# The numerators of six tile pairs move from the banks of the queries and transposes to the banks of the row maxima

## The chip, the core and the metric

The kernel runs on one core of a Trainium2 chip. A core has a matrix engine (TensorE, in the profile PE, with its weight loads as PEld), a vector engine (VectorE, DVE), a scalar engine (ScalarE, ACT), a general engine (GpSimd, POOL) and a queue that issues transfers (SyncE, SP). Each engine works through its own list of instructions in order, and waits at an instruction until the semaphores that it names are set. TensorE writes its products into accumulator tiles of 128 partitions by 512 f32 values, called banks here; ScalarE and VectorE read them out.

The metric is device time in microseconds (us) of one execution. Of the kernel before there are three runs: 979.75, 980.02 and 980.48 us.

## The reference: what is computed

Two attention layers work on the same 2048 tokens of 448 features, with 16 heads of 28 features, and a gate per token mixes them:

```python
g = sigmoid((x * gate_w).sum(-1, keepdims=True))
a = A(x)     # linear attention with a learned feature map
b = B(x)     # ordinary softmax attention
return g * a + (1 - g) * b
```

Layer A turns each query and key by a 28 x 28 matrix per head and takes softmax of the result and of its negative, which gives 56 features. With these, `kv = phi_k^T v` and `z = sum(phi_k)` are formed once per head; the output of a query is the numerator `phi_q kv` divided by the denominator `phi_q z`, and goes through `wo`. Layer B is softmax(q k^T / sqrt(28)) v, also through its `wo`.

## The kernel before

The work goes through stages, all in f32; products that need the precision are built from a high and a low part in the faster f32r format.

1. Projection of layer B's queries and keys, written to DRAM (`proj_qk`), up to about 100 us.
2. Key stage of layer A: for each of 16 tiles of 128 tokens, keys, features and values, and their sum over tokens in `pkv`.
3. Query stage of layer A, about 185 to 325 us. This is where the change lies.
4. Values of layer B (`value_b`), up to about 355 us.
5. Attention of layer B to the end: 256 steps of scores, exponentials and values.

Beside stages 2 to 4, TensorE also forms a part of layer B's scores in 80 units (`mx_unit`), only to find the largest score of each row: a softmax of layer B subtracts it later.

**The query stage.** One loop (`for i in range(2 * NT + 11)`) goes over the tiles; `q = i - 16` counts the query tiles and `y = q - 1`. The engines PE, DVE, ACT and POOL run in exactly the order in which the code issues; the order of SP's transfers is chosen by a planner when the program is built. In one turn of the loop these steps matter, in this order on TensorE:

- `pq`: the projection of query tile q, 11 products into one bank (`tok_major`, called at line 127 or 109 of the profile; here 109). ScalarE copies it out as `pcq` (L421). VectorE and GpSimd make the features `featq` from it.
- `mx_unit()` for q of 0, 1 and from 8 on: four products (L260, `pmd` and `pmb`, two of each) into four banks. ScalarE takes the positive part of the two `pmd` banks into `rl` (L264), and VectorE adds the two `pmb` banks to these and takes the maximum (L265). The two `pmd` banks are free after L264, the two `pmb` banks after L265.
- `numer(tb)` in every second turn, for tile pair tb = 0 to 7 (q = 5, 7, ..., 19): 32 small products (L529) into two banks `pn_0` and `pn_1`, written in turns: the first product goes to `pn_0`, the second to `pn_1`, and so on. ScalarE copies both out as `oUa` (L381, in `normalize1`).
- `turn`: eight transposes `pft` of features (L516) into two banks, copied out by ScalarE as `fT` (L519).
- `out_a`: 12 products `poa` (L109) for an earlier tile, copied out by ScalarE as `ga` (L544) and sent to DRAM as `gad` (L545). The order of `turn` and `out_a` changes late in the stage.

A numerator's division takes several turns: a small transfer `dena` (L384) collects the denominators from `oUa`, VectorE inverts them (L389), two small transfers write them to DRAM as `rda` (L393), and one of 512 KB spreads them over the partitions as `rsa` (L394). VectorE multiplies (L400), ScalarE and GpSimd split the result into `oTa` (L408, L409), which `poa` reads.

**The banks.** In the query stage there is one pool of banks, `psq`, with two rotations of four each:

```python
def ps_s(nm):
    return ps.tile([P, 512], F32, tag="s", name=nm, bufs=psn[0])
def ps_mx(nm):
    return ps.tile([P, 512], F32, tag="mx", name=nm, bufs=psn[1])
```

`psn` is 4 and 4 in this stage. The rotation `s` serves `pq`, `pft`, `pn`, `poa` and later `pvb`; the rotation `mx` serves only `mx_unit`, whose four tiles take all four of its banks, in the order pmd_0, pmd_1, pmb_0, pmb_1. A new tile takes the bank of the tile allocated four before it in its rotation, and its first product waits until that bank has been read out.

Of the kernel before, what the change touches and what calls it, by code (L numbers as in the profile page):

```python
# [41 lines left out]
def gated_mix_kernel(ctx, tc, xT, wqkB, wvB, wvA, wkAT, wqAT, phi, woA, woB,  # L42
# [20 lines left out]
    def ps_s(nm):  # L63
        return ps.tile([P, 512], F32, tag="s", name=nm, bufs=psn[0])
# [312 lines left out]
    def normalize1(pool, pn, nm, n):  # L377

        oU = pool.tile([P, n, 512], F32, tag="oU", name=f"oU{nm}", bufs=2 * n - 1)
        for i in range(n):  # L380
            (nc.scalar.copy if n == 2 else nc.vector.tensor_copy)(oU[:, i, :], pn[i])  # L381
        den = pool.tile([P, n, 16], F32, tag="den", name=f"den{nm}", bufs=2)
        for i in range(n):
            nc.sync.dma_start(den[:, i, :], oU[DH:P:32, i, :])  # L384
        return oU, den
# [135 lines left out]

    def numer(tb):

        pn = [ps_s(f"pn{tb}_{i}") for i in range(2)]
        for k in range(2):
            for j in range(4):
                for e in range(2):
                    es = slice(64 * e, 64 * e + 2 * DH + 1)
                    nc.tensor.matmul(pn[e][32 * j:32 * j + 32, k * 256:(k + 1) * 256],  # L529
                                     KV[es, k, 32 * j:32 * j + 32], fT_of[tb][es, 4 * k + j, :],  # L530
                                     start=True, stop=True, tile_position=(64 * e, 32 * j))
        num[tb] = normalize1(ta, pn, f"a{tb}", 2)
# [170 lines left out]
    for i in range(2 * NT + 11):  # L703
        t, q = i, i - NT
        y = q - 1
        tb = y // 2
# [80 lines left out]
        if y >= 4 and y % 2 == 0 and tb - 2 < 8:  # L787
            numer(tb - 2)
# [455 lines left out]
```

## Time and profile before

| | |
|---|---|
| median of three runs | 980.02 us (979.75 to 980.48) |
| the profiled execution | 979.64 us |
| its span in the trace | 977.9 us |
| PE busy | 970.2 us (99%) |
| ACT busy | 751.8 us (77%) |
| DVE busy | 715.9 us (73%) |
| POOL busy | 227.4 us (23%) |

Times in the trace are counted from the start of the span. A row of the timeline names its start, its length, engine, line, operation, what it writes and reads, and how many instructions it merges; in square brackets stands the idle time of that engine just before, and what ended it. The end of a product is modelled, so a short wait of TensorE is seen best at its weight loads (PEld): each product has a weight load of its own, in the same order.

### The profile page before, as it was taken

The page shows a single profiled execution, that of the slowest core. Times are in us where ns is not written, and L with a number is a line of the kernel's source. Part 1 is how long each engine was busy: PE and PEld are TensorE (multiplying, and loading weights), DVE is VectorE, ACT ScalarE, POOL GpSimd, SP SyncE. Part 2 cuts the span into 40 slices and gives each one's busy share as a digit, 9 for nine tenths or more (in the row PEclk, how much of TensorE's full clock was granted, in tenths as well). Part 3 has the DMA queues.
Part 4 walks back from the last instruction along what each step waited for, and adds up shares of the span by engine and source line. Part 5 has one row for each costly group of instructions (what it writes and reads, how often), then busy time and mean ns, then how long its engine had stood idle before and what let it go on. Part 6 is the DMA issues. An engine that isn't in the chain of part 4 may idle for free.

```text
span 977.9 us, 22543 instructions
## 1 busy us (share of the span) xinstructions
PE 970.2 (99%) x8510; PEld 600.8 (61%) x8510; DVE 715.9 (73%) x1338; ACT 751.8 (77%) x1442; POOL 227.4 (23%) x236
## 2 busy tenths in 40 slices
PE   9999999999999999999999999999999999999998
PEld 8877877787777655555555555555555555555555
DVE  5566767789745678888888888888888888885112
ACT  4455655578865689888898898988989889887662
POOL 1135435577634800021011001011011011010010
PEclk9999999999999999999999999999999999999999
DMA  9873110112243333022132121122231222100441
GB/s 305 310 256 113 39 53 33 37 52 82 75 114 108 98 112 132 29 59 50 60 91 73 33 61 47 59 77 72 65 83 45 63 60 64 42 21 32 142 151 57
DMA packets 56140, 84.49 MB, mean 86 GB/s; under 512 B 17216, under 2 KB 23984, under 8 KB 56032
## 3 DMA queue, kind: packets, MB, share of 16 engines
q1 hardware_dynamic: 56032, 83.06, 28.0%
q8 instruction: 67, 1.10, 0.5%
q14 instruction: 41, 0.34, 0.1%
HBM read 54.86 MB, written 27.78 MB: 85 GB/s over the span
## 4 chain that ended last, share of the span: by engine, by line
PE 93%; DMA 3%; DVE 2%; issue 1%; ACT 1%; SPq 1%; POOL 0%; DVEq 0%; POOLq 0%; ACTq 0%
PE g L863 29%; PE pv L1008 27%; PE pqk L109 5%; PE pk L127 4%; PE pva L127 4%; PE g L288 3%; PE poa L109 3%; PE pmd L260 3%; PE pob L109 3%; PE pq L109 3%; PE pvb L127 2%; PE pvb L109 2%; DMA rsa<-rda 2%; PE pqk L630 1%; PE pkv L468 1%
## 5 line engine op out<-in xcount | busy, mean ns | idle before, releaser
L871 ACT ACTIVATE p<-g 128x512 f32<-128x512 f32 x1020 | 525.6, 608 | 82.7 <-PE g L863 82.4
L295 DVE TENSOR_REDUCE part<-g 128x1 f32<-128x512 f32 x704 | 442.2, 683 | 84.0 <-PE g L288 82.8
L863 PEld LDWEIGHTS g<-qst,kst 32*128 32x128 f32 x3060 | 220.8, 182 | 215.5 <-DVE part L295 194.9
L863 PE MATMUL g<-qst,kst 32*128 32x512 f32 x3060 | 337.6, 419 | 0.1
L1008 PE MATMUL pv<-p,vb 128*32 128x512 f32 x2048 | 273.0, 604 | 0.0
L288 PE MATMUL g<-kc,qc 28*128 28x512 f32 x704 | 233.3, 494 | 0.0
L265 DVE CUSTOM_DVE_ANT_0 rl<-pmb,rl 128x512 f32<-128x512 f32 x160 | 103.3, 683 | 50.0 <-ACT rl L264 50.0
L400 POOL TENSOR_TENSOR oUb<-oUb,rsb 128x512 f32<-128x512 f32 x15 | 19.3, 1288 | 489.5 <-DMA rsb<-rdb 453.9
L264 ACT ACTIVATE rl<-pmd 128x512 f32<-128x512 f32 x160 | 87.4, 602 | 31.1 <-PE pmb L260 29.4
L288 PEld LDWEIGHTS g<-kc,qc 28*128 28x128 f32 x704 | 86.2, 181 | 0.2
L1008 PEld LDWEIGHTS pv<-p,vb 128*32 128x32 f32 x2048 | 40.5, 108 | 66.2 <-issue 64.9
L109 PE MATMUL pqk<-XH,wB 128*128 128x512 f32 x192 | 59.1, 396 | 0.0
L568 ACT CAST ev<-pqk 128x512 fp32r<-128x512 f32 x28 | 16.0, 589 | 39.1 <-PE pqk L109 23.0
L1019 DVE SCALAR_TENSOR_TENSOR acc<-pob,gate,acc 128x448 f32<-128x448 f32 x12 | 8.2, 683 | 48.4 <-PE pob L109 48.4
L109 PE MATMUL poa<-woA_s,oTa 128*128 128x448 f32 x192 | 43.5, 375 | 0.0
L260 PE MATMUL pmb<-kp,qp 28*128 28x512 f32 x160 | 41.7, 495 | 0.4
L569 DVE TENSOR_TENSOR ev<-pqk,ev 128x512 fp32r<-128x512 f32 x28 | 19.0, 690 | 30.4 <-ACT ev L568 30.3
L109 PEld LDWEIGHTS pqk<-XH,wB 128*128 128x128 f32 x192 | 35.4, 188 | 8.6 <-issue 1.5
L260 PE MATMUL pmd<-kp,qp 28*128 28x512 f32 x160 | 39.9, 494 | 0.0
L127 PE MATMUL pk<-wkA_s,XH 128*128 128x448 f32 x128 | 39.4, 381 | 0.0
L109 PEld LDWEIGHTS poa<-woA_s,oTa 128*128 128x128 f32 x192 | 34.8, 188 | 6.6 <-issue 2.6
L109 PE MATMUL pq<-wqA_s,XH 128*128 128x448 f32 x128 | 37.4, 375 | 1.4 <-ACT oUa L381 1.4
(158 smaller groups left out, 1053.9 us busy)
## 6 DMA issues: line engine op xcount, KB each, us to landing
qkd<-ev SPq DMA_DIRECT2D x28, 512.0 KB
qst<-qkd SPq DMA_DIRECT2D x64, 112.0 KB
kst<-qkd SPq DMA_DIRECT2D x64, 112.0 KB
od<-oTb SPq DMA_DIRECT2D x48, 112.0 KB
rsa<-rda SPq DMA_DIRECT2D x8, 512.0 KB
oL<-od SPq DMA_DIRECT2D x8, 512.0 KB
rsb<-rdb SPq DMA_DIRECT2D x15, 256.0 KB
gad<-ga SPq DMA_DIRECT2D x16, 224.0 KB
```

Of the source, the lines that this page charges most:

```text
L109: nc.tensor.matmul(dst, l, r, start=i == 0, stop=i == len(todo) - 1)
L127: nc.tensor.matmul(dst[:, :n], l, r, start=i == 0, stop=i == len(todo) - 1, skip_group_check=True)
L260: nc.tensor.matmul(pm[j], qc[js, qt * P:(qt + 1) * P], kc[js, :], start=True, stop=True, tile_position=(32 * i, 0))
L264: nc.scalar.activation(rl, pm[i], AF.Relu)
L265: nc.vector.tensor_tensor_reduce(rl, pm[2 + i], rl, 1.0, LOWEST, ALU.add, ALU.max, part[:, col + i:col + i + 1])
L288: nc.tensor.matmul(pm, mxs[("qc", gq)][js, qt * P:(qt + 1) * P], mxs[("kc", gq // NQ, kb)][js, :], start=True, stop=True, tile_position=(3 ...
L295: nc.vector.tensor_reduce(part[:, col:col + 1], pm, AX.X, ALU.max)
L400: (nc.gpsimd if n == 1 else nc.vector).tensor_mul(oU, oU, rs)
L569: nc.vector.tensor_sub(e[:, 1, :], pq, f32(e[:, 0, :]))
L863: nc.tensor.matmul(st[j], kst_of[(gq // NQ, kt // 4)][js, k, (kt % 4) * P:(kt % 4 + 1) * P], qst_of[gq][js, q, :], start=n == 0, stop=n == ...
L871: nc.scalar.activation(p, st[j], AF.Exp, scale=SCALE)
L1008: nc.tensor.matmul(pv[32 * j:32 * j + 32, :], vb[kt // 8][:, kt % 8, 4 * g + j, :], pt[j], start=kt == 0, stop=kt == NT - 1, tile_position ...
```

## The change

The two numerator banks of pairs 0 to 5 are taken from the rotation `mx` instead of `s`; those of pairs 6 and 7 stay in `s`.

```diff
     def numer(tb):
 
-        pn = [ps_s(f"pn{tb}_{i}") for i in range(2)]
+        pn = [(ps_mx if tb < 6 else ps_s)(f"pn{tb}_{i}") for i in range(2)]
         for k in range(2):
             for j in range(4):
                 for e in range(2):
```

The instructions and their order on PE, DVE, ACT and POOL are the same in both programs; their waits differ. On SP the planner changes the order of some transfers of pairs 2 to 5: for pairs 2, 3 and 4 `rsa` is issued ahead of a `gad` that it stood behind, and for pair 3 both `dena` follow the `rda` of pair 2 instead of enclosing them. The two numerator tiles advance the rotation `mx` by two, so the next unit's `pmd` tiles take the banks of the `pmb` tiles of the unit before, and its `pmb` tiles those of the numerators.

## The prediction

> **What bounds the kernel.** I read the page first, then the windows by stage, then TensorE's waits in the query stage, and last the timelines of PEld, PE and ACT around each numerator.
>
> ```profile
> PE 970.2 (99%) x8510; PEld 600.8 (61%) x8510; DVE 715.9 (73%) x1338; ACT 751.8 (77%) x1442; POOL 227.4 (23%) x236
> ...
> PE 93%; DMA 3%; DVE 2%; issue 1%; ACT 1%; SPq 1%; POOL 0%; DVEq 0%; POOLq 0%; ACTq 0%
> ```
> ```profile
> 200.00:283.00 83.00, 81.04 (x674) 63.81 (x672) 63.63 (x131) 66.26 (x123) 54.30 (x52) 1.00 0.23 68
> ```
>
> TensorE is busy 99% of the span, 93% of the chain that ended last is its own work, and in the stretch of the eight numerators (columns PE, PEld, DVE, ACT, POOL, granted clock, DMA share, GB/s) 81.04 of 83.00 us at the full granted clock of 1.00. So a microsecond that TensorE waits here is a microsecond of the end, unless a later wait shrinks by it. What it waits for, seen at its weight loads from 200 to 283 us (total us, times, longest):
>
> ```profile
> PEld pq L109 <- ACT oUa L381: 2.0, 3, 1.1
> ...
> PEld pvb L109 <- ACT fT L519: 0.8, 1, 0.8
> ...
> PEld pmb L260 <- DVE part L265: 0.8, 2, 0.4
> ...
> PEld poa L109 <- POOL oTa L409: 0.3, 1, 0.3
> ```
>
> The first row is what the change can remove: a query's product waits for the bank of a numerator that ScalarE has not copied yet. Behind the stage, the only wait of PE itself is this one, from 283 us to the end:
>
> ```profile
> PE pvb L109 <- ACT ga L544: 0.3, 1, 0.3
> ```
>
> It hangs on a chain that TensorE itself starts, so a delay made in the query stage is carried to the end.
>
> **What it removes.** The waits, one by one, at the weight loads:
>
> ```profile
> 206.13 0.30 PEld L109 LDWEIGHTS pq<-wqA_s,XH 128*128 128x128 f32 x2 [0.18 <-ACT oUa L381]
> ...
> 214.34 0.30 PEld L109 LDWEIGHTS pq<-wqA_s,XH 128*128 128x128 f32 x2 [0.79 <-ACT oUa L381]
> ...
> 223.82 0.30 PEld L109 LDWEIGHTS pq<-wqA_s,XH 128*128 128x128 f32 x2 [1.06 <-ACT oUa L381]
> ...
> 276.35 0.30 PEld L109 LDWEIGHTS pvb<-wvB_s,XH 128*128 128x128 f32 x2 [0.83 <-ACT fT L519]
> ```
>
> The first three follow pairs 0, 1 and 2 (the last row belongs to a later step). With the numerators out of the rotation `s`, a turn allocates there only pq and two pft (and poa later), so the bank four back is one that was read a turn earlier: all three go, 0.18 + 0.79 + 1.06 = 2.03 us. No row shows such a wait behind pairs 3 to 7, where poa stands between numerator and query; moving pairs 3, 4 and 5 can gain nothing of this kind.
>
> **What it adds.** From pair 2 on a row-maximum unit stands directly ahead of each numerator on TensorE:
>
> ```profile
> 220.45 0.50 PE L260 MATMUL pmd<-kp,qp 28*128 28x512 f32 x2
> 220.46 0.49 PE L260 MATMUL pmb<-kp,qp 28*128 28x512 f32 x2
> 220.88 1.09 PE L529 MATMUL pn<-fT,KV 57*32 57x256 f32 x32
> 221.91 1.09 PE L516 MATMUL pft<-ident,featq 128*128 128x128 f32 x8
> ...
> 231.51 1.09 PE L529 MATMUL pn<-fT,KV 57*32 57x256 f32 x32
> ...
> 245.10 1.09 PE L529 MATMUL pn<-fT,KV 57*32 57x256 f32 x32
> ...
> 258.49 1.09 PE L529 MATMUL pn<-fT,KV 57*32 57x256 f32 x32
> ```
>
> The unit fills all four banks of `mx`, and 0.43 us later (220.88 less 220.45) the numerator begins. After the change its two tiles take the banks of the unit's own pmd_0 and pmd_1, which ScalarE frees with the two activations of L264:
>
> ```profile
> 221.33 1.13 ACT L264 ACTIVATE rl<-pmd 128x512 f32<-128x512 f32 x2
> ...
> 231.90 1.10 ACT L264 ACTIVATE rl<-pmd 128x512 f32<-128x512 f32 x2
> ...
> 245.25 1.09 ACT L264 ACTIVATE rl<-pmd 128x512 f32<-128x512 f32 x2
> ...
> 258.65 1.09 ACT L264 ACTIVATE rl<-pmd 128x512 f32<-128x512 f32 x2
> ```
>
> In the built program the first product of pn_0 and that of pn_1 both wait on ScalarE. The second product of the block goes to pn_1, so 31 of the 32 stand behind the end of the second activation: 222.46, 233.00, 246.34 and 259.74, which is 1.58, 1.49, 1.24 and 1.25 us after the starts of today. TensorE resumes soon after a copy ends. One oUa takes 597 ns, so the first of the row at 213.72 ends at 214.32, and pq above starts at 214.34, on PE after an idle time shown as 0.55:
>
> ```profile
> L381 ACT COPY oUa<-pn x16: 570/597/684, 205.5 to 280.9; 128x512 f32<-128x512 f32 x16
> ...
> 213.72 1.06 ACT L381 COPY oUa<-pn 128x512 f32<-128x512 f32 x2
> ...
> 260.46 1.08 ACT L381 COPY oUa<-pn 128x512 f32<-128x512 f32 x2
> ```
> ```profile
> 214.34 0.67 PE L109 MATMUL pq<-wqA_s,XH 128*128 128x448 f32 x2 [0.55 <-ACT oUa L381]
> ...
> 263.04 0.50 PE L260 MATMUL pmd<-kp,qp 28*128 28x512 f32 x2
> ```
>
> That is 0.02 us; I add 0.05, as one such row is little to go by, and take off 0.03 for the one product that goes ahead (1.09 us for 32): new stalls of 1.60, 1.51, 1.26 and 1.27, together 5.64 us. From below, if only the first activation (0.60 us) held the block back, they would be 1.05 + 0.99 + 0.75 + 0.76 = 3.55. From above, weight loads that must begin anew cost at most the 0.24 us by which PEld's wait exceeds PE's at 214.34 (0.79 against 0.55), four times, 0.96 in all: 6.6. I take 5.64, because both waits stand in the program and the restart was seen. Queued behind the stalled product is all of TensorE's list: pft, poa and the next pq, and so ScalarE's fT and ga and the features. Pairs 0 and 1 cost nothing: no unit runs between q = 2 and q = 7, so the banks are empty. The next unit's waits change to L265 of the unit before and to oUa. The tightest is pair 5: its oUa ends at 261.54, 1.50 us ahead of the next unit at 263.04, and the stall moves both; I put it at nothing, with that 1.50 as cover, and if the cover were gone it would cost what oUa is late.
>
> **What absorbs or gives back.** Two pieces of the chain in order of time do not start at the numerators' stalls:
>
> ```profile
> 217.48 8.94 DMA rsa<-rda
> ...
> 226.51 0.46 DVE oUa L400
> ...
> 231.09 0.50 PE pmb L260
> 231.58 1.02 PE pn L529 x32
> 232.61 2.84 PE poa L109 x12
> ...
> 246.19 2.65 PE poa L109 x12
> ...
> 263.88 0.41 SPq L545
> ...
> 264.40 9.09 DMA rsa<-rda
> 273.50 0.02 issue
> 273.52 1.24 DVE oUa L400
> ...
> 276.35 2.49 PE pvb L109 x11
> ```
>
> First, the unit ahead of pair 3 waits for VectorE, which waits for pair 0's transfer; that chain goes back to pq at 206.13 and can move only by its 0.18. So whatever TensorE has won by then beyond 0.18 is lost there (ScalarE's pmd activations of that unit, at 231.90, come behind oTa of the same transfer and move with it). The following poa took 2.84 against 2.65 us since it waited for GpSimd; if it comes later, 0.19 goes. Second, pvb at 276.35 waited 0.83 us (0.8 in the list of waits) for a chain through pair 4's rsa. That chain starts ahead of pair 5's stall (VectorE's inverse follows the unit, not the numerator), and in the new order of SP rsa no longer stands behind gad (the SPq piece at 263.88). Pair 5's stall of 1.27 moves TensorE but not this transfer, so the wait of 0.83 goes.
>
> The running sum, as TensorE's delay against today: -0.18, -0.97 after pair 1's pq; +1.60 - 1.06 gives -0.43 after pair 2; held to -0.18 at 231.09; +1.51 makes 1.33; -0.19 at poa 1.14; +1.26 makes 2.40; +1.27 makes 3.67; -0.83 at pvb leaves **2.84 us**. The profiled execution took 979.64 us and becomes 982.5; it stood 0.38 below the median, so the median of 980.02 becomes 982.9.
>
> [...]
>
> **Rivals.**
>
> *Faster: the banks are a reserve and the activations are done in time.* The three waits go, no new one comes: 980.02 - 2.03 = 978.0. It decides if L264 ends before the numerator is reached, 1.24 to 1.58 us earlier than now. Against it: the activation needs the unit's own product, 0.43 us before the numerator, and two take 1.09. For it: only the empty turns of pairs 0 and 1. Chance 0.05. [...]
>
> *No difference: the stall lasts for the first activation only*, because the products of pn_0 run on while pn_1's bank is read, or other engines catch up. The running sum is then -0.97 + 1.05 - 1.06, held to -0.18, + 0.99 - 0.19 + 0.75 + 0.76 - 0.83 = 1.30: 981.3. For it: the two banks are freed one after the other; against it: an engine's list is in order. Chance 0.15.
>
> *Slower by more: nothing is given back.* If pvb still waits its 0.83, poa its 0.19, and the three stalls behind 231.09 cost 0.24 more each, 2.84 + 0.83 + 0.19 + 0.72 = 4.58: 984.6. For it: the margin at pvb is small, since ScalarE must still do two L264 and oTa before fT. Chance 0.12.
>
> *The change does something else:* numerators take the pmb banks and wait for VectorE's L265 in place of ScalarE. At pair 2 that unit's second L265 ran here:
>
> ```profile
> 223.17 0.68 DVE L265 CUSTOM_DVE_ANT_0 rl<-pmb,rl 128x512 f32<-128x512 f32 x1
> ```
>
> It ends at 223.85, 1.39 us after ScalarE's 222.46; three such stalls count behind 231.09, 4.2 us more: 987.1. The rotation by allocation order speaks against it. Chance 0.02.
>
> **How the numbers follow.** My forecast, four stalls of ScalarE's making and 2.84 us more, has chance 0.66. A measurement of this kernel tells about 0.2% (1.96 us) from no change. The forecast, the third and the fourth rival are slower: 0.80; the second is the same: 0.15; the first faster: 0.05. The range runs from 980.8, half a microsecond below the second rival, to 985.0, just past the third, which leaves out the first, the fourth and the far sides; the forecast's own range is 982.6 to 983.7: 0.25 lower if pair 0's transfer moves with TensorE after all, 0.83 higher if pvb gives nothing back.
>
> **What would show it.** Right: no wait of pq for oUa at the weight loads; four new waits of pn on rl L264, 1.2 to 1.6 us each, at pairs 2 to 5 and none at 0 and 1; the wait of pvb for fT gone; the same busy times; everything from 283 us on moved by one constant of 2 to 4 us. Wrong: waits of pn under 0.8 us, waits on part L265, a unit waiting for oUa, or a new wait in the attention stage. The prediction fails above all if some wait that I took as fixed, the transfer of pair 0 or the chain to pvb, moves otherwise.

## The result and the profile after

| | before | after |
|---|---|---|
| median (lowest to highest) | 979.63 us (978.63 to 980.48), 6 executions | 984.13 us (982.26 to 986.78), 6 executions |
| the profiled execution, its span | 979.64 us, 977.9 us | 983.56 us, 981.7 us |
| mean granted clock of TensorE, execution by execution | 1.000 in the one profiled | 1.000 at 982.26; 0.998 at 983.56, 984.13, 984.14 and 985.34; 0.997 at 986.78 |

The ratio is 1.0048 with a 95% interval of 1.0033 to 1.0064: slower by 4.5 us, a little over twice what can be told from no change. The forecast was 982.9. The one execution that kept the full clock lies near it, and the other five above.

First the page of the kernel after (its row of engines), then its windows (PE, PEld, DVE, ACT, POOL, granted clock, DMA share, GB/s):

```profile
PE 971.8 (99%) x8510; PEld 602.7 (61%) x8510; DVE 716.4 (73%) x1338; ACT 752.0 (77%) x1442; POOL 227.0 (23%) x236
```
```profile
200.00:283.00 83.00, 78.89 (x624) 62.41 (x623) 61.97 (x126) 63.87 (x118) 53.78 (x51) 0.98 0.20 65
...
232.60:233.10 0.50, 0.50 (x22) 0.11 (x7) 0.50 (x3) 0.29 (x1) 0.50 (x1) 0.87 0.26 107
233.10:233.60 0.50, 0.50 (x8) 0.39 (x2) 0.50 (x3) 0.24 (x1) 0.50 (x2) 0.50 0.24 74
...
236.00:236.50 0.50, 0.50 (x3) 0.46 (x2) 0.50 (x2) 0.00 (x0) 0.50 (x1) 0.61 0.14 16
236.50:237.00 0.50, 0.50 (x5) 0.45 (x4) 0.50 (x1) 0.00 (x0) 0.50 (x1) 1.00 0.10 12
```

The other engines' busy times are the same to 0.5 us; TensorE's grew by 1.6, though its instructions are the same. The numerator stretch shows two things: TensorE is busy 2.15 us less in it (78.89 against 81.04), so it waits more, and its clock is 0.98 instead of 1.00, so some of its products take longer. The small windows find the low clock in one place. At 0.87 and 0.61 in the windows at its ends, it was 0.50 from 232.97 to 236.39, that is for 3.4 us. Half a clock for 3.4 us of a span of 981.7 is a mean of 0.998.

TensorE's waits at the weight loads from 200 to 287 us, in the kernel after:

```profile
PEld pn L529 <- ACT rl L264: 6.7, 8, 1.8
...
PEld pmb L260 <- DVE part L265: 0.4, 1, 0.4
```

and, from the timeline of its weight loads:

```profile
220.57 0.13 PEld L529 LDWEIGHTS pn<-fT,KV 57*32 57x32 f32 x2 [1.38 <-ACT rl L264]
...
221.05 0.61 PEld L529 LDWEIGHTS pn<-fT,KV 57*32 57x32 f32 x30 [0.35 <-ACT rl L264]
...
229.66 0.18 PEld L260 LDWEIGHTS pmb<-kp,qp 28*128 28x128 f32 x1 [0.43 <-DVE part L265]
231.61 0.13 PEld L529 LDWEIGHTS pn<-fT,KV 57*32 57x32 f32 x2 [1.77 <-ACT rl L264]
...
247.80 0.13 PEld L529 LDWEIGHTS pn<-fT,KV 57*32 57x32 f32 x2 [1.05 <-ACT rl L264]
...
262.47 0.14 PEld L529 LDWEIGHTS pn<-fT,KV 57*32 57x32 f32 x2 [1.05 <-ACT rl L264]
...
280.00 0.39 PEld L109 LDWEIGHTS pvb<-wvB_s,XH 128*128 128x128 f32 x2
```

The waits of `pq` for `oUa` are gone, and so is that of `pvb` for `fT`. Pairs 2 to 5 each wait for L264, in two pieces: the weight loads of two products go behind the first activation, and the other 30 wait for the second (0.35 more). Pairs 0 and 1 don't wait. At pair 3 TensorE stands longest, 1.77 us, just behind a unit of four short products. Right behind it the clock drops (at 232.97), and `poa` pays. In the chain of the kernel after:

```profile
233.29 4.08 PE poa L109 x12
...
249.38 2.65 PE poa L109 x12
```

The first of these lies in the stretch at half clock: 1.43 us more than the second. Its weight loads show no wait for GpSimd or for a transfer.

The profile after stands in the table below, step by step: the start of each of TensorE's blocks against the same block of before. The stage itself began 0.41 us earlier in this execution, and that is taken off. (The first 100 us scatter from one execution to the next: the stage began between 0.41 us earlier and 2.61 us later in the profiles of this study, the 2.61 in the one that was at half clock for 3.4 us between 60 and 65 us too.)

| step | predicted, us | measured, us |
|---|---|---|
| wait of pq behind pair 0 | -0.18 | -0.21 |
| behind pair 1 | -0.79 | -0.83 |
| pair 2: stall | +1.60 | +1.61 |
| wait of pq behind it | -1.06 | -1.08 |
| running sum at the unit ahead of pair 3 | -0.18 (held there) | -1.02 |
| pair 3: stall | +1.51 | +2.10 |
| running sum behind it | 1.33 | 1.08 |
| poa behind it | -0.19 | **+1.25** |
| pair 4: stall | +1.26 | +1.27 |
| pair 5: stall | +1.27 | +1.29 |
| wait of pvb | -0.83 | -0.82 |
| running sum at pvb | 2.84 | 4.06 |

From the next unit on the sum is 4.20, and it stays within 0.2 of that to the end of the span: less the 0.41 it is the 3.8 us by which the span grew. Without the 1.43 us of the half clock the 4.20 would be 2.77.

### The profile page after: what moved, and what is told of

Same layout as the page of the kernel before. It is cut to its first block, busy times and chain, and to the rows that moved or that the text cites. A ratio compares the mean times of both kernels' runs of the same rounds, so it can differ in the third digit from the quotient of the medians.

```text
span 981.7 us, 22538 instructions
## 1 busy us (share of the span) xinstructions
PE 971.8 (99%) x8510; PEld 602.7 (61%) x8510; DVE 716.4 (73%) x1338; ACT 752.0 (77%) x1442; POOL 227.0 (23%) x236
## 4 chain that ended last, share of the span: by engine, by line
PE 76%; ACT 0%; DVE 0%; issue 0%
PE g L863 29%; PE pv L1008 27%; PE poa L109 4%; PE g L288 3%; PE pob L109 3%; PE pvb L127 2%; PE pvb L109 2%; PE pmd L260 2%; PE pq L109 1%; PE pft L516 1%; PE poL L1041 1%; PE pn L529 1%; PE poL L1118 0%; ACT rl L264 0%; ACT oTa L408 0%; PE st L863 0%
## 5 line engine op out<-in xcount | busy, mean ns | idle before, releaser
L265 DVE CUSTOM_DVE_ANT_0 rl<-pmb,rl 128x512 f32<-128x512 f32 x160 | 103.4, 684 | 52.9 <-ACT rl L264 52.9
L264 ACT ACTIVATE rl<-pmd 128x512 f32<-128x512 f32 x160 | 87.4, 602 | 31.1 <-PE pmb L260 30.1
L127 PE MATMUL pva<-wvA_s,XH 128*128 128x450 f32 x128 | 37.8, 372 | 0.0
```

The lines of the kernel that those rows point to most:

```text
L127: nc.tensor.matmul(dst[:, :n], l, r, start=i == 0, stop=i == len(todo) - 1, skip_group_check=True)
L264: nc.scalar.activation(rl, pm[i], AF.Relu)
L265: nc.vector.tensor_tensor_reduce(rl, pm[2 + i], rl, 1.0, LOWEST, ALU.add, ALU.max, part[:, col + i:col + i + 1])
```

## The experiments

All of them compute the whole reference. Each is held against runs of the kernel before on the same chip. "Clock low" counts the executions whose mean granted clock is below 0.999; the kernel before had 3 such among 67. "At full clock" is the median of the others. Where in an execution the clock was low is seen only in its profile, and each kernel of the table has one.

| kernel | median, us | beside it, before | ratio, 95% interval | clock low | at full clock, us |
|---|---|---|---|---|---|
| pairs 0, 1 moved | 980.36 | 979.24 | 1.0009 (0.9999 to 1.0019) | 6 of 11 | 979.31 |
| pair 2 moved | 979.06 | 979.24 | 0.9994 (0.9985 to 1.0003) | 1 of 12 | 978.96 |
| pair 3 moved | 982.10 | 979.24 | 1.0023 (1.0013 to 1.0034) | 9 of 12 | 979.55 |
| pairs 4, 5 moved | 982.20 | 979.24 | 1.0028 (1.0018 to 1.0039) | 1 of 8 | 982.07 |
| after, split of wvB a turn earlier | 985.10 | 979.05 | 1.0061 (1.0046 to 1.0077) | 6 of 6 | none |
| before, the same | 980.17 | 979.05 | 1.0004 (0.9996 to 1.0013) | 0 of 11 | 980.17 |
| after, unit behind out_a2 | 984.24 | 979.05 | 1.0054 (1.0038 to 1.0070) | 4 of 6 | 982.52 |
| before, the same | 984.92 | 979.05 | 1.0060 (1.0048 to 1.0073) | 4 of 5 | 983.37 |
| after, pair 3 in `s` | 983.45 | 979.41 | 1.0036 (1.0022 to 1.0050) | 4 of 6 | 981.52 |
| after, numerators 3 to 5 behind out_a2 | 981.65 | 979.41 | 1.0020 (1.0012 to 1.0029) | 4 of 11 | 980.87 |
| before, the same | 982.57 | 979.41 | 1.0030 (1.0017 to 1.0043) | 5 of 6 | 980.83 |
| pairs 0, 1 moved, once more | 980.77, one execution | 979.41 | | 1 of 1 | none |

### Each part of the change alone

```diff
-        pn = [ps_s(f"pn{tb}_{i}") for i in range(2)]
+        pn = [(ps_mx if tb < 2 else ps_s)(f"pn{tb}_{i}") for i in range(2)]          # pairs 0, 1
+        pn = [(ps_mx if tb == 2 else ps_s)(f"pn{tb}_{i}") for i in range(2)]         # pair 2
+        pn = [(ps_mx if tb == 3 else ps_s)(f"pn{tb}_{i}") for i in range(2)]         # pair 3
+        pn = [(ps_mx if tb in (4, 5) else ps_s)(f"pn{tb}_{i}") for i in range(2)]    # pairs 4, 5
```

> Only pairs 0 and 1 take the banks of the row maxima. Theory (bank waits, with the unit ahead of pair 3 held by pair 0's transfer): the waits of pq for oUa of 0.18 and 0.79 us go, that of 1.06 behind pair 2 stays, no numerator waits for an activation; of the 0.97 won, 0.2 to 1.0 survives at the unit ahead of pair 3, so 0.2 to 1.0 us faster than before, and the granted clock stays 1.000. Rival (the running sum is additive and nothing holds the gain): 0.97 faster. Rival (these waits cover others that take their place): within 0.1 of before.

> Only pair 2 takes the banks of the row maxima. Theory: its numerator waits 1.6 us for the activations, the wait of pq behind it (1.06) goes, and the 0.5 that is left over is taken up wholly or in part by the wait of the next-but-one unit for pair 0's transfer (0.77 at the weight loads): 0 to 0.5 us slower. Rival (no absorption): 0.54 slower. If one stall of 1.6 us is enough for the granted clock to fall, up to 1.7 more in part of the runs.

> Only pair 3 takes the banks of the row maxima. Theory (stall plus a halved clock behind it): the numerator waits 1.5 us (the sum goes by 1.51 less 0.19 at poa: 1.3 slower), and where the granted clock falls to 0.50 behind it, as it did for 3.4 us in the changed kernel, about 1.4 more; so executions lie in two groups, 1.3 and 2.7 slower than before, with a mean clock of 1.000 and 0.998. Rival (the long poa of the changed kernel, 4.08 against 2.65 us, came from GpSimd or the transfers, not the clock): all runs 2.7 slower and poa long at a clock of 1.00. Rival (the clock falls only after several stalls): all runs 1.3 slower at 1.000.

> Only pairs 4 and 5 take the banks of the row maxima. Theory: two stalls of 1.26 and 1.27 us (1.30 each in the changed kernel's trace), and pvb gives back its wait of 0.83: 1.7 us slower, the wait of pvb for fT gone. Rival (nothing given back, the transfer moves along): 2.5 slower, the wait of pvb still there. The clock at 1.000 if stalls of 1.3 us are too short to lower it; otherwise single runs 1 to 2 us above the others.

*Pairs 0 and 1.* The two waits go (1.04 us in its profile), and 0.92 of it is still there at the unit ahead of pair 3. In that execution the gain lasts to the end, but the stage had begun 1.06 us later than in the profile before, so the times are the same. At full clock no gain is measured: 979.31 against 979.24. The median is 980.36, against an expected gain of 0.2 to 1.0, since 6 of 11 executions have a lower clock.

*Pair 2.* The stall of 1.75 us at the weight loads (1.4 and 0.35) less the wait behind it leaves +0.52 us at the next unit in its profile, and 0.58 behind it: not absorbed at the unit that waits for VectorE. From about 300 us on only 0.3 is left, as `pvb` no longer waits for `ga` there. In the times no difference is established.

*Pair 3.* Here the clock was low in 9 of 12 executions, down to 0.996. The profiled one kept it, and its timeline of weight loads shows the bare stall:

```profile
230.12 0.18 PEld L260 LDWEIGHTS pmb<-kp,qp 28*128 28x128 f32 x1 [0.18 <-DVE part L265]
230.73 0.18 PEld L260 LDWEIGHTS pmb<-kp,qp 28*128 28x128 f32 x1 [0.43 <-DVE part L265]
232.36 0.14 PEld L529 LDWEIGHTS pn<-fT,KV 57*32 57x32 f32 x2 [1.44 <-ACT rl L264]
232.84 0.61 PEld L529 LDWEIGHTS pn<-fT,KV 57*32 57x32 f32 x30 [0.35 <-ACT rl L264]
```

Behind it the delay is 1.51 us, as forecast, and 1.32 behind `poa`. Against the expectation `pvb` lost its wait for `fT` here too, which left 0.60, and from about 300 us on 0.2. The three executions at full clock took 979.46, 979.55 and 980.97, the other nine 982.28 in their median: what pair 3 costs lies in the clock more than in the stall.

*Pairs 4 and 5.* Two stalls of 1.29 us each in its profile, and `pvb` gave back 0.82: +1.76, and +2.00 at the end. The profiled execution, 982.07, is also the median at full clock, 2.8 us above before. Of these, 2.0 are the sum at the end and 0.4 the stage's later start; the profiled execution of before lay another 0.4 above the median here. The clock stayed up in 7 of 8 executions, though these stalls too are over a microsecond.

### Is it pair 3's stall that lowers the clock?

Taken out of the change, pair 3 has no stall. If that stall alone were the cause, the clock would stay up.

```diff
-        pn = [(ps_mx if tb < 6 else ps_s)(f"pn{tb}_{i}") for i in range(2)]
+        pn = [(ps_mx if tb in (0, 1, 2, 4, 5) else ps_s)(f"pn{tb}_{i}") for i in range(2)]
```

> The changed kernel with pair 3 back in the banks of the queries (pairs 0, 1, 2, 4 and 5 stay with the row maxima). Theory (pair 3's stall, the longest and next to the unit's wait for VectorE, is what lets the granted clock fall): most executions at 0.999 or 1.000; no stall of pair 3 (1.5 to 2.1 us) and no halved clock (1.4), while pairs 4 and 5 still cost 1.29 each less 0.83 at pvb, and pairs 0 to 2 give 0.4 back, so 0.9 to 1.8 us slower than before, 2.5 to 4 faster than the changed kernel. Rival (any of the stalls, or the number of them, lowers the clock): mean clock 0.998 as in the changed kernel, 2.5 to 3.5 slower than before.

It was low in 4 of 6 executions, the profiled one among them. Its weight loads, and its windows:

```profile
231.99 0.18 PEld L260 LDWEIGHTS pmb<-kp,qp 28*128 28x128 f32 x1 [1.20 <-DVE part L265]
...
232.60 0.18 PEld L260 LDWEIGHTS pmb<-kp,qp 28*128 28x128 f32 x1 [0.43 <-DVE part L265]
```
```profile
232.00:234.00 2.00, 1.88 (x34) 0.84 (x34) 1.93 (x6) 2.00 (x6) 2.00 (x3) 1.00 0.29 104
234.00:236.00 2.00, 2.00 (x14) 1.73 (x7) 2.00 (x6) 2.00 (x5) 2.00 (x2) 0.58 0.25 102
236.00:238.00 2.00, 2.00 (x8) 1.77 (x7) 1.93 (x7) 0.31 (x1) 1.90 (x3) 0.57 0.10 18
```

TensorE stood 1.63 us for VectorE, which came late behind the transfer `rsa` of pair 0: from its issue to VectorE's multiplication it took 9.39 us here, against 8.05 in the profile after. So pair 3's stall is not needed, and this theory falls. (The kernel is 4.0 us slower than before, more than theory and rival gave.) The kernel with pairs 0 and 1 moved gives the closest comparison: one program, profiled twice, with the clock up in the first and low in the second.

> Pairs 0 and 1 alone once more, for a second profile: of eleven executions five had a mean clock of 1.000 and six of 0.996 to 0.998. Theory (TensorE reaches the unit ahead of pair 3 about 1 us sooner and, where the transfer of pair 0 takes its usual 8.9 us or more, waits there 1 us longer, which lowers the clock): an execution with a clock below 0.999 shows a wait of pmb for L265 of 1.5 us or more near 230 us and 0.50 right behind it; one at 1.000 shows a wait under 1 us. Rival (the clock falls elsewhere, in the projections): the low stretch lies ahead of 100 us.

Weight loads of the first execution, then of the second, then windows of the second:

```profile
230.61 0.18 PEld L260 LDWEIGHTS pmb<-kp,qp 28*128 28x128 f32 x1 [0.46 <-DVE part L265]
231.22 0.18 PEld L260 LDWEIGHTS pmb<-kp,qp 28*128 28x128 f32 x1 [0.43 <-DVE part L265]
```
```profile
230.57 0.18 PEld L260 LDWEIGHTS pmb<-kp,qp 28*128 28x128 f32 x1 [1.49 <-DVE part L265]
231.19 0.18 PEld L260 LDWEIGHTS pmb<-kp,qp 28*128 28x128 f32 x1 [0.43 <-DVE part L265]
```
```profile
230.00:232.00 2.00, 1.31 (x10) 0.59 (x18) 2.00 (x5) 2.00 (x5) 2.00 (x3) 0.88 0.26 84
232.00:234.00 2.00, 2.00 (x33) 0.90 (x18) 1.93 (x6) 2.00 (x5) 2.00 (x3) 0.50 0.28 98
234.00:236.00 2.00, 2.00 (x9) 1.80 (x9) 2.00 (x6) 0.90 (x2) 2.00 (x3) 0.77 0.20 72
```

The stage began 1.06 us later in the first execution, while VectorE's multiplication started at the same time (226.66 and 226.63), as the transfer took 8.14 us in the first and 9.17 in the second. So the unit waited 0.89 us in the one and 1.92 in the other, and behind the longer wait the clock fell to half: the signs that were expected. The rival fell for this execution alone; another kernel below was also at half clock for 3.4 us between 60 and 65 us, in the projections. The gain of pairs 0 and 1 brings TensorE earlier to a transfer that doesn't come earlier: it turns into idle time, and the idle time can cost clock.

### Can the stall be moved away?

Three moves, each made in the kernel after and in the kernel before. The first takes the casts of `wvB` out of ScalarE's list ahead of pair 3's activations:

```diff
-        if q in (8, 10):
-            split_part(wvB_s, "wvB", D, (q - 8) // 2)
+        if q in (7, 9):
+            split_part(wvB_s, "wvB", D, (q - 7) // 2)
```

> The changed kernel with the two casts of wvB (L143, 0.94 us each on ScalarE, and the subtraction L144 of VectorE) moved from q = 8 and 10 to q = 7 and 9. Theory (ScalarE reaches the activations of pairs 2 and 3 late because of these casts, its list having no idle time from pq to the activation): the stalls of pairs 2 and 3 fall from 1.73 and 2.12 at the weight loads to about 1.4 each, all four are alike, and with the longest wait gone the granted clock falls less often or not at all: 1.0 to 2.5 us faster than the changed kernel, 2 to 3.5 slower than before. Rival (the clock falls by chance with any such stall): the stalls are shorter but the mean clock stays at 0.998 and the gain is 0.5 to 1.0.

> The kernel before with the same move of the casts, as a control. Theory: the unit ahead of pair 3 no longer has L144 in its chain (1.08 us behind the transfer of pair 0), so its wait of 0.77 at the weight loads goes; ScalarE copies pair 2's oUa at about the same time: 0 to 0.8 us faster than before. Rival: L144 now delays VectorE where it is busiest (8.8 of 10 us at 200 to 220), and a new wait of equal size comes: 0 to 0.5 slower.

In the kernel after the waits for L264 sank only from 6.7 to 6.1 us (longest 1.5), and the unit now waited 1.2 us for VectorE (longest 0.7). A stretch of 6.8 us at half clock followed, twice as long as in the profile after, and the clock was low in all 6 executions. The expected gain didn't come: part of the wait moved to VectorE. In the kernel before the unit's wait for VectorE went, as expected, but the waits of `pq` for `oUa` grew from 2.0 to 3.4 us, and no difference in time is established. Its two longest waits are these, each between eight transposes and a `pq`, all on 128 rows:

```profile
216.21 0.30 PEld L109 LDWEIGHTS pq<-wqA_s,XH 128*128 128x128 f32 x2 [1.62 <-ACT oUa L381]
...
226.18 0.30 PEld L109 LDWEIGHTS pq<-wqA_s,XH 128*128 128x128 f32 x2 [1.56 <-ACT oUa L381]
```

Each is longer than the longest wait ahead of the low clock with pairs 0 and 1 moved (1.49), and yet none of 11 executions had a low clock.

The second issues the unit behind `out_a2`, so that `poa` stands between it and the next numerator:

```diff
-        if q in (0, 1) or q >= 8:
+        if q in (0, 1) or q >= 8 and q not in (9, 11, 13, 15):
             mx_unit()
...
             out_a2(y - 10)
+        if q in (9, 11, 13, 15):
+            mx_unit()
```

> The changed kernel with the row-maximum unit of q = 9, 11, 13 and 15 issued behind the transposes or poa that follow the numerator, not directly ahead of it. Theory (the numerator stalls only since the unit has just filled the banks): no numerator waits for rl L264, the clock stays at 1.000, the waits of pq for oUa stay away, the unit's pmb finds oUa already copied: 0.5 to 2 us faster than before, 5 to 6 faster than the changed kernel. Rival (the wait only moves: the unit now waits for oUa by 0.5 to 1 us each): 0 to 2 us slower than before.

> The kernel before with the same move of the unit, as a control. Theory: the unit ahead of pair 3 comes 3 us later and no longer waits for VectorE (0.77); the waits of pq for oUa (2.03 in all) stay or shrink a little, as ScalarE copies oUa without two activations ahead of it: 0.3 to 1.5 us faster than before. If it is as fast as the changed kernel with the same move, the banks are worth nothing once the unit stands there. Rival: the later unit delays VectorE's work for the features, 0 to 1 us slower.

The waits for L264 are gone, but the next units wait for VectorE (2.9 us in all) and for `oUa` (1.2). The longest of them in the kernel after:

```profile
228.26 0.18 PEld L260 LDWEIGHTS pmb<-kp,qp 28*128 28x128 f32 x1 [1.86 <-DVE part L265]
```

Its clock is at half from about 230.6 to 234 us. The kernel before has 3.7 us of such waits after the move, the longest 2.7, and 4 of 5 executions with a low clock: again the clock falls behind a long idle time around 230 us, whatever ends it. Its profile has a second such stretch, in the projections: a mean of 0.66 from 60 to 65 us is 3.4 us at half clock, behind 5 us in which TensorE was idle for 0.56 (windows in the columns used above):

```profile
55.00:60.00 5.00, 4.44 (x21) 2.70 (x19) 3.39 (x7) 3.00 (x5) 2.79 (x2) 1.00 0.49 159
60.00:65.00 5.00, 4.84 (x12) 3.46 (x13) 2.42 (x7) 1.19 (x2) 0.72 (x2) 0.66 0.59 220
```

The two kernels are 5.2 and 5.9 us slower than before. Both were expected to be faster, and the rivals, at most 2 and 1 us slower, missed too.

The third issues the numerators of pairs 3 to 5 behind `out_a2` instead:

```diff
-        if y >= 4 and y % 2 == 0 and tb - 2 < 8:
+        if y >= 4 and y % 2 == 0 and tb - 2 < 8 and y not in (10, 12, 14):
             numer(tb - 2)
...
             out_a2(y - 10)
+        if y in (10, 12, 14):
+            numer(tb - 2)
```

> The changed kernel with the numerators of pairs 3, 4 and 5 issued behind poa in place of ahead of it, so that 2.4 us of poa stand between the unit and the numerator. Theory (the stall is only the time from the unit to the end of its two activations): the stalls of pairs 3, 4 and 5 go and only pair 2's is left; clock at 1.000 in most runs; the gains of pairs 0 to 2 keep 0.4 to 1 us; pvb's wait of 0.8 is back: 0 to 1 us faster than before, 4 to 5 faster than the changed kernel. Rival (the wait moves on: the next unit's pmb waits for oUa, or poa for GpSimd): 0.5 to 2 slower than before.

> The kernel before with the same move of the numerators, as a control. Theory: without poa between the numerator and the next pq, pq waits for oUa behind pairs 3, 4 and 5 as it does behind pairs 0 to 2 (0.2 to 1.1 each): 0.6 to 3 us slower than before, and 1 to 3 slower than the changed kernel with the same move. Rival (ScalarE has copied oUa in time): within 0.3 of before.

In the kernel after, three of the four stalls go, and 2.5 us with them (981.65). What takes their place is a wait of `poa` for GpSimd's half of `oTa`, seen at its weight loads:

```profile
233.08 0.50 PEld L109 LDWEIGHTS poa<-woA_s,oTa 128*128 128x128 f32 x3 [0.69 <-POOL oTa L409]
234.32 1.32 PEld L109 LDWEIGHTS poa<-woA_s,oTa 128*128 128x128 f32 x7 [0.74 <-POOL oTa L409]
```

This is the wait that the rival named; the kernel is 2.2 us slower than before. In the kernel before I had expected waits of `pq` behind pairs 3 to 5 once `poa` no longer stands between; none came (2.0 us in 3, as without the move). It is 3.2 us slower all the same, with the same wait of `poa` for GpSimd (1.4 us in 2) and a low clock in 5 of 6 executions. With this order the two placements of the banks take 980.87 and 980.83 us at full clock, the second from a single execution, so no difference is established. None of these kernels is faster than the kernel before.

## Why the prediction was right, and where it was off

**What bounds the kernel**: as read. Both a wait and a slower product of TensorE in this stage went through to the end of the profile after. It is not so in every case: with pair 2 or pair 3 alone moved, `pvb` no longer waited for `ga` at about 300 us, and 0.4 us of the delay was given back there.

**What it removes**: three waits of `pq`, 0.21, 0.83 and 1.08 us, each within 0.04 of the forecast.

**What it adds**: four stalls at pairs 2 to 5, held by the second activation of the unit directly ahead. Three of them came within 0.03 us, and the copying row plus 0.02 was a good price for the restart. The second rival (first activation only) fell: the weight loads of 30 of the 32 products stood behind the second. The fourth (VectorE's banks) fell too: no numerator waited for L265.

**Held to -0.18 at 231.09**: mis-sized. The step took pair 0's transfer to last 8.94 us again. In the profile after, the row of its issue on SP and that of VectorE's multiplication, which ended its wait with it, are:

```profile
217.06 0.53 SPq L394 DMA_DIRECT2D rsa<-rda  x1
```
```profile
225.11 1.23 DVE L400 TENSOR_TENSOR oUa<-oUa,rsa 128x1024 f32<-128x1024 f32 x1 [0.98 <-DMA rsa<-rda]
```

That is 8.05 us, against 9.03 measured the same way in the profile before, and TensorE kept its lead (-1.02). The step also let the activations of pair 3 move with the unit. They did not: the unit came 1.02 us earlier, their end 0.54, and the stall grew to 2.10 in place of 1.51. That the two errors nearly cancel behind it (1.08 against 1.33) is luck. That TensorE's gain is lost when the transfer is long is shown by the program with pairs 0 and 1 moved, where the unit waited 1.92 us in one execution. From issue to multiplication the profiles of this study have 7.8 to 9.6 us: one profile is not enough to take this time as fixed.

**-0.19 at poa**: this is the step that failed, and with it an assumption that the sum never named, that the granted clock stays at 1.00. Where the clock stayed up, behind pairs 4 and 5 and behind pair 3 when it was moved alone, `poa` took 2.65 us, as the forecast has it; here it took 4.08. Without that 1.43 the 4.20 would be 2.77, within 0.1 of the forecast's 2.84. The median is 1.2 us over the forecast, where five of six executions had a low clock, and the one at full clock (982.26) lies 0.6 below it. So the median lies above the forecast's own range of 982.6 to 983.7. It lies in the wide range, up to 985.0, because that made room for the upper rival, nothing given back, which fell (`pvb` gave its 0.82): that part is luck.

**-0.83 at pvb**: right in size. The reason given (only pair 5's stall moves TensorE against the transfer, helped by the new order on SP) is not shown: the wait went as well where pair 3 alone was moved, and it stayed where only pairs 0 and 1 or pair 2 were. What the order on SP contributes wasn't tried by itself.

**The faster rival**: it fell, as from pair 2 on the banks were full, and four numerators waited for them, 6.7 us in all at the weight loads. Where they are empty they do serve as a reserve: pairs 0 and 1 alone lose two waits, 1.04 us. But no gain in time is measured (979.31 at full clock against 979.24, and a median above that). The executions at full clock are no fair sample either, if the clock falls where the stage begins early, as in the two profiles of that kernel. So how much the two waits are worth stays open.

## What to carry to other kernels

A bank is free for a tile only if whatever fills it ahead is already read out: look at what the engine runs directly before, and add the copying time to the path where it is a unit that fills the whole rotation (here two activations of 0.60 us each, and stalls of 1.27 to 2.10 us). Taking away a wait ahead of a wait that doesn't move can gain nothing, and where it makes one idle time of TensorE out of several small ones, it can cost the clock as well: with pairs 0 and 1 moved 1.04 us of waits went, the time at full clock was 979.31 us against 979.24 before, and behind a wait of 1.92 us the clock was 0.50. So where a change gathers idle time in one place, look up the granted clock there, and compare several executions of it before pricing the change by one.

## What the runs showed of the hardware

I had not expected the granted clock to fall behind so short an idle time. In the profile after it was 0.50 for 3.4 us, following idle times of 0.43, 1.77 and 0.35 us at the weight loads within 3 us, between short products on 28 or 57 rows. In the program with pairs 0 and 1 moved, idle times of 1.49 and 0.43 us were followed by the drop, and 0.46 and 0.43 were not. In the profile after the idle times sum to 2.55 us, in the other to 1.92, both less than the low stretch behind them. That stretch was 3.4 us long in the other profiles that have one, too, but for 6.8 us in the kernel after with the casts moved.

How much idle time it takes stays open, and it isn't the idle time alone: 1.62 and 1.56 us between products on 128 rows left the clock at 1.00 (the kernel before with the casts moved). From 200 us to the last product, every stretch at half clock in these profiles follows a unit that waited for VectorE (0.43 to 2.69 us at one weight load), with its products on 28 rows; whether the small products are what counts wasn't tried by itself. The same kind of stall (1.37 and 0.35 us at pair 2, 1.05 and 0.36 at pairs 4 and 5) stood in kernels with a low clock in 1 of 12 and in 1 of 8 executions, at pair 3 (1.44 and 0.35, with the unit's waits shortly ahead) in 9 of 12.

Beyond the two profiles with pairs 0 and 1 moved, what makes one execution of a program differ from the next is not shown. TensorE's busy time just ahead doesn't decide alone either: in the 3.4 us ahead of the drop it was 1.9 us in the profile after and 2.4 in that with pair 3 in `s`. In the kernel before with the casts moved, a stretch of 3.4 us that holds the whole of the wait ending at 216.21 us has 2.0 us of it, and no drop followed.

The f32r products were the faster ones in the profile before, by columns and between products of different shapes: from the start of one block to the start of the next, twelve `poa` of 448 columns took 2.65 us, 0.49 ns a column, and eight transposes in f32 of 128 columns 0.87 us, 0.85 ns a column.
